# Attention over memory and a feed-forward layer on one core: maxima over tokens without a transposed phi, v behind a weight block, another order table

## The chip, the core and the metric

The kernel runs on one core of a Trainium2 chip. A core has five engines that run their own instruction streams and meet through semaphores: PE (TensorE, matmuls; its weight loads are shown as PEld), DVE (VectorE), ACT (ScalarE), POOL (GpSimd) and SP, which here only issues DMAs. The metric is the device time of one execution in microseconds (us); less is better.

## What is computed

The inputs are q, k, v of shape (8 batches, 8 heads, 576 tokens, 64) and phi of shape (8, 8, 576, 32), all float32 values, and two weights w_in (512 x 2048) and w_out (2048 x 512) that arrive as 8-byte floats.

```
a = exp(phi - max over tokens of phi); a = a / (sum over tokens of a + 1e-9)
k_m = a^T k; v_m = a^T v                       (32 memory rows per head)
attn = softmax over the 32 rows of (q k_m^T / 8)
x = attn v_m, laid out as 4608 tokens x 512
h = x @ w_in; g = h * cos(h); out = g @ w_out
```

## The kernel before

**What is multiplied.** x is never formed. For each batch the kernel folds v_m into w_in (`fold`, `fold_first`, tiles pv, pvf, vf, vw), so that h is attn times the folded weight. `gemm1` makes one 128-row piece of h for a group of 384 tokens (tile hp, L730 for the first group in float32, L739 for the others in float16 pairs), `act` and `act_end` turn it into g (tiles u and gp), `gemm2` multiplies by w_out and sums in three accumulators (tile acc, L776 for the first group, L781 for the others). There are 12 groups of 384 tokens and 16 pieces f per group. PSUM has three buffers for hp, three for acc and two small ones that everything else takes in turn.

**What prepares a batch.** `memory(b)` subtracts the maxima from phi, takes exp, and multiplies with k and v (tile psA, 40 matmuls that use 32 columns of the array); `attend(b)` makes the scores (tile sc), their softmax and its transpose (tile aT). Batch 0 has its own `memory_first`, which first makes k_m (psk), and then v_m (psv, X_v, tpx_v, vm) from a separate load of v.

**The maxima.** There are two ways. For batches 4 to 7 `maximum(b)` (L344 to L353) takes elementwise maxima over the token blocks on DVE, and POOL's `partition_all_reduce` then gives every partition the maximum over all of them. Batches 1 to 3 (`NT = 4`) load a second, transposed copy of phi (tile phiT, 576 KB, L208), DVE reduces it along tokens (nmx, L452), and two PE matmuls spread the result over the partitions (tile top, L455).

**The weights.** They arrive in 8 blocks each (`load_w_in`, `load_w_out`, 1 MB a block). `to_float32` rebuilds a float32 block from the bits of 8-byte floats: a cast of the upper halves on ACT (L277), then one DVE operation that ors in the lower bits (L280), then a square sum on ACT (L283) for the scale. `convert_next` does one or more of these blocks at each step f of group 0, so the first 100 us carry this work beside the matmuls.

**The order.** The program is written in loops, but each engine's stream is reordered at the end: `NEXT` holds one string per engine, and each number says which of the instructions not yet issued comes next. The order of every engine, and that of SP's DMA issues, is therefore a table of numbers. An engine waits at an instruction whose inputs aren't ready, and everything behind it in its table waits too.

PE starts with filler matmuls on zeros (tile warm, L833, 43 of them), which are placed in the opening by the same table.

Of the kernel before, what the change touches and what calls it, by code (L numbers as in the profile page):

```python
# [11 lines left out]
F32 = mybir.dt.float32  # L12
# [32 lines left out]
NT = 4  # L45
# [50 lines left out]
    mybir.EngineType.Activation: (  # L96
# [907 lines left out]
```

## Time and profile before

| | |
|---|---|
| median of 3 runs | 678.17 us (677.82 to 681.54) |
| profiled execution, its own time | 677.69 us |
| its span from first to last instruction | 675.8 us |
| PE busy | 664.4 us, 98% |
| DVE busy | 517.8 us, 77% |
| ACT busy | 496.0 us, 73% |
| POOL busy | 19.9 us, 3% |
| HBM read, written | 51.79 MB, 9.44 MB |

An engine's busy time says how much of the span its units ran, not whether somebody waited for it. The 1.9 us between the span and the execution's own time lie outside the instructions.

### The profile page before, as it was taken

What the parts mean: (1) busy time and instruction counts of PE and PEld (TensorE: products, weight loads), DVE (VectorE), ACT (ScalarE), POOL (GpSimd) and SP (SyncE); (2) the same over time, 40 slices, a digit from 0 to 9 for tenths busy, and PEclk for the clock granted to TensorE, in tenths of its full rate; (3) what the DMA queues carried; (4) which work ended last, traced back from release to release, by engine and by line L of the source; (5) the groups of instructions that cost most, each with busy time, mean ns of one, the idle gap of its engine ahead of it and who ended that gap; (6) DMA issues with size and microseconds to landing.
All of it is one profiled execution on the core that took longest, in us unless ns stands there. A gap on an engine that the chain in (4) does not pass through costs nothing.

```text
span 675.8 us, 12557 instructions
## 1 busy us (share of the span) xinstructions
PE 664.4 (98%) x4959; PEld 345.8 (51%) x4959; DVE 517.8 (77%) x1124; ACT 496.0 (73%) x921; POOL 19.9 (3%) x26
## 2 busy tenths in 40 slices
PE   7799999999999999999999999999999999999997
PEld 3343455564454445665454545655445445665543
DVE  5868799999999877788669877688766766766553
ACT  1798889988878967776866868776775776756553
POOL 4001100000000000000000000000000000000000
PEclk9999999999999999999999999999999999999999
DMA  8997780016143000630027000520000000001001
GB/s 296 396 342 275 241 294 1 18 52 217 42 165 99 32 1 1 194 102 16 1 60 233 18 1 32 179 85 1 32 16 16 17 1 32 16 1 48 16 16 63
DMA packets 25290, 62.03 MB, mean 92 GB/s; under 512 B 2256, under 2 KB 8720, under 8 KB 23184
## 3 DMA queue, kind: packets, MB, share of 16 engines
q1 hardware_dynamic: 20768, 53.24, 23.0%
q10 hardware_dynamic: 4464, 8.00, 3.2%
q8 instruction: 39, 0.64, 0.4%
q14 instruction: 19, 0.16, 0.1%
HBM read 51.79 MB, written 9.44 MB: 91 GB/s over the span
## 4 chain that ended last, share of the span: by engine, by line
PE 97%; ACT 1%; DVE 1%; issue 0%
PE acc L781 51%; PE hp L739 26%; PE acc L776 6%; PE pv L667 3%; PE hp L730 3%; PE psA L479 2%; PE sc L582 2%; PE warm L833 1%; PE pvf L676 1%; PE pv L676 1%; PE psA L485 0%; ACT w_in_sb L277 0%; DVE w_in_sb L200 0%; PE psk L387 0%; PE tpx L503 0%; PE top L455 0%
## 5 line engine op out<-in xcount | busy, mean ns | idle before, releaser
L781 PE MATMUL acc<-wo,gp 128*128 128x512 f16 x1584 | 372.8, 379 | 0.0
L781 PEld LDWEIGHTS <-gp 128*128 128x128 f16 x1584 | 151.2, 98 | 170.6 <-issue 13.9
L739 PE MATMUL hp<-aT,vw 128*128 128x192 f16 (+1 forms) x1440 | 199.0, 283 | 0.0
L739 PEld LDWEIGHTS <-vw 128*128 128x128 f16 x1440 | 130.2, 98 | 71.2 <-issue 5.6
L750 ACT ACTIVATE gp<-hp,cu 128x192 int32<-128x192 f32 (+1 forms) x240 | 115.4, 491 | 59.9 <-PE hp L739 26.5
L751 DVE SCALAR_TENSOR_TENSOR u<-hp,cu,gp 128x192 f32<-128x192 f32 (+1 forms) x240 | 119.1, 504 | 45.4 <-ACT gp L750 43.5
L756 ACT ACTIVATE u<-u,quarter 128x384 f32<-128x384 f32 x192 | 116.2, 612 | 41.4 <-DVE u L751 40.3
L760 DVE SCALAR_TENSOR_TENSOR u<-hp,u 128x384 f32<-128x384 f32 x176 | 96.2, 551 | 36.6 <-ACT u L756 35.3
L763 DVE TENSOR_TENSOR gp<-u,gp 128x384 f16<-128x384 f32 x176 | 95.7, 549 | 27.3 <-ACT gp L762 26.7
L762 ACT CAST gp<-u 128x384 f16<-128x384 f32 x176 | 87.1, 506 | 28.5 <-DVE u L760 25.3
L776 PE MATMUL acc<-wo,gp 128*128 128x512 f32 x96 | 45.5, 603 | 0.0
L683 DVE SCALAR_TENSOR_TENSOR vw<-pv,vw 128x512 f16<-128x512 f32 x48 | 32.5, 683 | 5.9 <-ACT vw L682 5.9
L682 ACT ACTIVATE vw<-pv 128x512 f16<-128x512 f32 x48 | 27.8, 592 | 5.3 <-PE pv L667 5.1
L776 PEld LDWEIGHTS acc<-wo,gp 128*128 128x128 f32 x96 | 17.1, 190 | 20.5 <-issue 17.2
L756 ACT ACT_TABLE_LOAD x20 | 25.7, 1283 | 0.4
L730 PE MATMUL hp<-aT,vf 128*128 128x384 f32 x64 | 24.1, 501 | 0.8 <-DVE aT L613 0.8
L805 ACT ACTIVATE ob<-acc,os 128x512 f32<-128x512 f32 x27 | 18.4, 687 | 4.5 <-PE acc L781 4.0
L588 DVE STREAM_TRANSPOSE at<-sc 128x288 f32<-128x288 f32 (+2 forms) x32 | 14.6, 468 | 4.3 <-PE sc L582 4.2
L730 PEld LDWEIGHTS hp<-aT,vf 128*128 128x128 f32 x64 | 11.3, 189 | 12.4 <-issue 2.6
L667 PE MATMUL pv<-w_in_sb,vp 64*32 64x512 f16 x432 | 15.8, 380 | 0.0
L582 PE MATMUL sc<-q,km 64*32 64x288 f32 (+2 forms) x256 | 14.7, 414 | 0.8 <-DVE vf L703 0.6
L833 PE MATMUL warm<-zeros 128*128 128x512 f16 x43 | 12.4, 425 | 2.3 <-DVE zeros L183 2.3
(159 smaller groups left out, 474.0 us busy)
## 6 DMA issues: line engine op xcount, KB each, us to landing
kv<-in_kv SPq DMA_DIRECT2D x28, 516.0 KB, 7.2
raw_out<-in_w_out SPq DMA_DIRECT2D x8, 1024.0 KB, 6.7
q<-in_qT SPq DMA_DIRECT2D x7, 1152.0 KB, 6.3
out<-ob ACTq DMA_DIRECT2D x30, 256.0 KB, 2.0
raw_in<-in_w_in SPq DMA_DIRECT2D x6, 1024.0 KB, 7.0
phi<-in_phi SPq DMA_DIRECT2D x8, 512.0 KB, 6.3
wo<-in_w_in SPq DMA_DIRECT2D x2, 1024.0 KB, 15.6
kv<-in_kv SPq DMA_DIRECT2D x14, 129.0 KB, 7.2
```

The lines of the kernel that those rows point to most:

```text
L667: nc.tensor.matmul(pv[g][M * c:M * (c + 1)], lhsT=st["vp", b][rows, vi, c], rhs=w2[rows, c, wi], start=(k == 0), stop=(k == 2), skip_group ...
L683: nc.vector.scalar_tensor_tensor(out=vw[:, 1, g], in0=src, scalar=T, in1=vw[:, 0, g], op0=ALU.mult, op1=ALU.subtract)
L730: nc.tensor.matmul(hp[:, :GT], lhsT=st["vf", q][:, g, fo * P:(fo + 1) * P], rhs=st["aTf"][:, g], start=(g == 0), stop=(g == 1))
L739: nc.tensor.matmul(hp[:, c0:c0 + n], lhsT=vw[:, wi, g, fo * P:(fo + 1) * P], rhs=aT[:, ai, g, c1:c1 + n], start=(k == 0), stop=(k == 5))
L750: nc.scalar.activation(ni[:, c], hp[:, c], AF.Copy, scale=cu, bias=0.25)
L751: nc.vector.scalar_tensor_tensor(out=u[:, c], in0=hp[:, c], scalar=cu, in1=ni[:, c], op0=ALU.mult, op1=ALU.subtract)
L756: nc.scalar.activation(u, u, AF.Sin, scale=TWO_PI_BELOW, bias=quarter)
L760: nc.vector.scalar_tensor_tensor(out=u, in0=hp[:, :GT], scalar=2.0 ** -17, in1=u, op0=ALU.mult, op1=ALU.mult)
L762: nc.scalar.copy(gp[:, 0], u)
L763: nc.vector.tensor_tensor(out=gp[:, 1], in0=u, in1=gp[:, 0], op=ALU.subtract)
L776: nc.tensor.matmul(accs[grp][t], lhsT=gp[:, t * P:(t + 1) * P], rhs=wo[:, f + 1], start=(f == 0), stop=(f == NF - 1))
L781: nc.tensor.matmul(accs[grp][t], lhsT=gp[:, gi, t * P:(t + 1) * P], rhs=parts[:, wi], start=(f == 0 and gi == 0 and wi == 0), stop=(f == N ...
```

## The change

The diff without the order tables, of which the first row of PE's stands for all (all five tables are new):

```diff
-NT = 4
 LAG = 4
 NEXT = {
     mybir.EngineType.PE: (
-        "0x26 8 0x16 1x8 2x8 3x8 6x2 18x5 6x2 7 6 7 6 0 6 5 9x4 0 8x9 0 7x6 9x16 0x14 1 2 0x3 1 0 14x2 6x6 7 "
+        "0x26 8 0x16 1x8 0x10 1x8 0x7 1 2 0 2 0x7 24x2 0x40 2x2 0x3 1 0 1 0x10 8x2 16 0x2 1 0x2 11 0x4 1 2 3 "
...
     def load_phi(b):
-        if 0 < b < NT:
-            loads["phiT", b] = t = ld.tile([P, 2, S], F32, tag="phiT", name=f"phiT_{b}", bufs=1)
-            nc.sync.dma_start(out=t, in_=phiT[b].rearrange("(g p) s -> p g s", p=P))
...
-        cast = nc.scalar.copy(top, upper)
+        cast = nc.scalar.copy(top, upper) if j > 0 else nc.vector.tensor_copy(out=top, in_=upper)
...
     def memory(b):
-        a = loads.pop(("phi", b))
-        if b < NT:
-
-            nmx = wk.tile([P, 2], F32, tag="nmx", name=f"nmx_{b}", bufs=1)
-            nc.vector.tensor_reduce(out=nmx, in_=loads.pop(("phiT", b)), op=ALU.max, axis=AX.X)
-            top = small_ps(f"top_{b}")[:, 0:HM]
-            for g in range(2):
-                nc.tensor.matmul(top[:, g * P:(g + 1) * P], lhsT=nmx[:, g:g + 1].broadcast_to([P, P]), rhs=ident,
-                                 start=True, stop=True)
-        else:
-            top = st["top", b]
-        yield
-        if b >= NT:
+        a = loads["phi", b]
+        if ("top", b) not in st:
+            maximum(b)
+        top = st["top", b]
+        loads.pop(("phi", b))
+        yield
+        if b > 1:
             yield
             yield
...
     load_q(0)
+    load_w_in(0)
     load_first(v_first, H * K1, H * KV)
-    load_w_in(0)
     load_w_in(1)
...
-            if i == e - 6 and NT <= b + 1 < B:
+            if i == e - 6 and ("phi", b + 1) in loads:
                 maximum(b + 1)
```

So all of batches 1 to 7 take `maximum(b)`; three DMAs, three DVE reductions and six PE matmuls go; three times four DVE operations and one all-reduce come. The cast of block 0 of each weight moves from ACT to DVE (`j > 0` is the condition for ACT). The load of w_in's block 0 is issued ahead of the five loads of the first batch's v.

**DVE around the first block of w_out.** The names: raw_in and raw_out are weight blocks as loaded, w_in_sb and wo the rebuilt ones, vf is the folded weight of batch 0 copied from its PSUM tile pvf, u and gp the activation of piece f of group 0. Before:

```order
L280 SCALAR_TENSOR_TENSOR w_in_sb<-raw_in_122,w_in_sb 128x4x256
L751 SCALAR_TENSOR_TENSOR u_0_391<-hp_0_388,gp_0_392 128x384
L703 COPY vf_315<-pvf_1_347 128x256
L280 SCALAR_TENSOR_TENSOR wo<-raw_out_125,wo 128x1024
L758 TENSOR_TENSOR gp_0_392<-hp_0_388,u_0_391 128x384
```

With the change:

```order
L275 SCALAR_TENSOR_TENSOR w_in_sb<-raw_in_122,w_in_sb 128x4x256
L740 SCALAR_TENSOR_TENSOR u_0_389<-hp_0_386,gp_0_390 128x384
L272 CAST wo<-raw_out_125 128x1024
L275 SCALAR_TENSOR_TENSOR wo<-raw_out_125,wo 128x1024
L692 COPY vf_315<-pvf_1_347 128x256
L747 TENSOR_TENSOR gp_0_390<-hp_0_386,u_0_389 128x384
```

The copy of vf, which frees a small PSUM buffer, stood ahead of the w_out block's work and now stands behind both of its operations.

**DVE at the maxima of batch 1.** phi is the block of batch 1, at the scores of batch 0, mx the maxima. With the change:

```order
L740 SCALAR_TENSOR_TENSOR u_2_466<-hp_2_463,gp_2_467 128x384
L342 TENSOR_TENSOR mx_434<-phi_360 128x512
L275 SCALAR_TENSOR_TENSOR w_in_sb<-wo,w_in_sb 128x4x256
L343 TENSOR_TENSOR mx_434<-mx_434 128x256
L346 TENSOR_TENSOR mx_434<-mx_434,phi_360 64x128 x2
L586 TENSOR_TENSOR at_232<-at_232,rm_233 128x384
L457 TENSOR_TENSOR phi_360<-phi_360,mx_434 64x128
L692 COPY vf_401<-pvf_1_452 128x512
L452 TENSOR_TENSOR phi_360<-phi_360,mx_434 128x1024
L457 TENSOR_TENSOR phi_360<-phi_360,mx_434 64x128
L747 TENSOR_TENSOR gp_2_467<-hp_2_463,u_2_466 128x384
```

The first subtraction from phi waits for POOL's all-reduce of mx, and the copy of vf, the large subtraction and the product gp of piece 2 stand behind it.

**PE at the memory products of batch 1.** hp are pieces of group 0, psA the products of phi with k and v, on 32 columns of the array. Before (the first 16 products stand ahead of these rows):

```order
L730 MATMUL hp_5_611<-aT_231,vf_403 128x384 x2
L479 MATMUL psA_0_473<-kv_2_370,phi_362 32x129 x4
L479 MATMUL psA_1_474<-kv_2_370,phi_362 32x129 x4
L479 MATMUL psA_1_474<-kv_3_372,phi_362 32x129 x4
L479 MATMUL psA_0_473<-kv_3_372,phi_362 32x129 x4
L485 MATMUL psA_0_473<-kv_4_374,phi_362 32x129 x2
L485 MATMUL psA_1_474<-kv_4_374,phi_362 32x129
L485 MATMUL psA_0_473<-kv_4_374,phi_362 32x129 x2
L485 MATMUL psA_1_474<-kv_4_374,phi_362 32x129
L730 MATMUL hp_6_647<-aT_231,vf_403 128x384 x2
L485 MATMUL psA_1_474<-kv_4_374,phi_362 32x129 x2
```

With the change:

```order
L719 MATMUL hp_5_610<-aT_231,vf_401 128x384
L468 MATMUL psA_0_472<-kv_0_364,phi_360 32x129 x4
L468 MATMUL psA_0_472<-kv_1_366,phi_360 32x129 x4
L468 MATMUL psA_0_472<-kv_2_368,phi_360 32x129 x4
L468 MATMUL psA_0_472<-kv_3_370,phi_360 32x129 x4
L474 MATMUL psA_0_472<-kv_4_372,phi_360 32x129 x4
L468 MATMUL psA_1_473<-kv_0_364,phi_360 32x129 x4
L468 MATMUL psA_1_473<-kv_1_366,phi_360 32x129 x4
L468 MATMUL psA_1_473<-kv_2_368,phi_360 32x129 x4
L468 MATMUL psA_1_473<-kv_3_370,phi_360 32x129 x4
L474 MATMUL psA_1_473<-kv_4_372,phi_360 32x129 x4
L719 MATMUL hp_6_646<-aT_231,vf_401 128x384 x2
```

The 40 products stood in three pieces with hp matmuls between them and now stand in one. In the same way the 16 score products of batch 1 go from three pieces to two, and the eight pvf products of the third quarter of w_in from two to one.

## Rows read from the trace of the kernel before

**Rows 1.** Page, busy time, share of the span and instructions per engine.

```profile
PE 664.4 (98%) x4959; PEld 345.8 (51%) x4959; DVE 517.8 (77%) x1124; ACT 496.0 (73%) x921; POOL 19.9 (3%) x26
```

**Rows 2.** Stretches: length, then PE, PEld, DVE, ACT, POOL busy; granted clock; DMA, GB/s.

```profile
20.00:25.00 5.00, 2.44 (x24) 0.91 (x22) 4.60 (x8) 3.43 (x7) 0.00 (x0) 1.00 1.04 417
35.00:40.00 5.00, 5.00 (x23) 2.45 (x29) 4.32 (x9) 4.76 (x10) 0.00 (x0) 1.00 1.06 337
40.00:50.00 10.00, 10.00 (x113) 4.78 (x100) 5.43 (x13) 8.92 (x15) 0.00 (x0) 1.00 0.92 353
```

**Rows 3.** Chain that ended last, 19 to 50 us: start, length, what.

```profile
26.82 1.24 ACT wo L277
...
30.29 0.55 PE sc L582 x14
...
32.33 1.29 PE warm L833 x6
...
37.49 0.44 PE top L455 x4
```

**Rows 4.** Timeline of the opening: start, busy us, what [idle before <-releaser].

```profile
2.30 4.83 PE L833 MATMUL warm<-zeros 128*128 128x512 f16 x14 [2.30 <-DVE zeros L183]
...
5.43 3.07 SPq L236 DMA_DIRECT2D kv<-in_v_first  x5
...
9.18 1.00 SPq L261 DMA_DIRECT2D raw_in<-in_w_in  x2
```

**Rows 5.** DMA issues at 8.0 to 9.7 us: size, us from issue to landing.

```profile
kv<-in_v_first SPq DMA_DIRECT2D x1, 128.0 KB, 7.5
...
raw_in<-in_w_in SPq DMA_DIRECT2D x1, 1024.0 KB, 10.0
```

**Rows 6.** Groups by line (L751: first 50 us): busy us, mean ns | idle before.

```profile
L277 ACT CAST wo<-raw_out 128x1024 f16<-128x1024 bf16 x8 | 10.8, 1347 | 0.0
L280 DVE SCALAR_TENSOR_TENSOR wo<-raw_out,wo 128x1024 uint32<-128x1024 uint32 x8 | 9.8, 1220 | 4.3 <-ACT wo L277 4.2
L200 DVE MEMSET w_in_sb<- 128x1024 f32 x3 | 2.7, 912 | 0.5 <-issue 0.5
L751 DVE SCALAR_TENSOR_TENSOR u<-hp,gp 128x384 f32<-128x384 f32 x6 | 3.2, 552 | 0.2 <-ACT gp L750 0.2
L703 DVE COPY vf<-pvf 128x256 f32<-128x256 f32 x2 | 0.8, 404 | 0.2 <-PE pvf L676 0.2
```

**Rows 7.** Groups by line and shape, the two ways to the maxima.

```profile
L452 DVE TENSOR_REDUCE nmx<-phiT 128x2 f32<-128x1152 f32 x3 | 4.0, 1332 | 0.0
L352 POOL PARTITION_ALL_REDUCE mx<-mx x4 | 4.3, 1072 | 95.4 <-DVE mx L351 95.4
```

**Rows 8.** Timeline of POOL, its first all-reduce.

```profile
50.58 0.35 POOL L441 PARTITION_ALL_REDUCE l<-l  x1 [41.88 <-DVE l L439]
```

**Rows 9.** Timeline of PE, 48 to 82 us: pieces on 32 columns.

```profile
48.69 0.41 PE L485 MATMUL psA<-kv,phi 64*32 64x129 f32 x4
...
53.52 0.71 PE L582 MATMUL sc<-q,km 64*32 64x288 f32 x16
...
55.02 1.14 PE L582 MATMUL sc<-q,km 64*32 64x288 f32 x14
...
58.94 0.67 PE L582 MATMUL sc<-q,km 64*32 64x288 f32 x2
...
61.45 1.08 PE L676 MATMUL pvf<-w_in_sb,vm 64*32 64x512 f32 x14
...
63.52 1.04 PE L676 MATMUL pvf<-w_in_sb,vm 64*32 64x512 f32 x2
...
80.41 1.09 PE L676 MATMUL pvf<-w_in_sb,vm 64*32 64x512 f32 x16
```

**Rows 10.** Timeline of PE, two whole fold groups of 24 matmuls.

```profile
183.35 0.84 PE L667 MATMUL pv<-w_in,vp 64*32 64x512 f16 x24
...
438.64 1.27 PE L667 MATMUL pv<-w_in_sb,vp 64*32 64x512 f16 x24
```

More of the change, by code (lines that the diff above doesn't have):

```diff
@@ L49 @@
     mybir.EngineType.PE: (
[46 rows of a table removed]
-    mybir.EngineType.Activation: (
[18 rows of a table removed]
-    mybir.EngineType.DVE: (
[24 rows of a table removed]
[44 rows of a table added]
+    mybir.EngineType.Activation: (
[18 rows of a table added]
+    mybir.EngineType.DVE: (
[25 rows of a table added]
     mybir.EngineType.Pool: (
-        "1 3x2 1x2 0x2 1x3 0x12 "),
+        "1 0x2 2 4 0 3 1 0 1x2 0x14 "),
     mybir.EngineType.SP: (
-        "0x36 6 0x2 4 0x3 1x2 0x9 3x2 0x8 3x2 0x8 3x2 0x8 3x2 0x8 3x2 0x14 "),
+        "0x35 6 0x3 3x2 0 2 0x8 3x2 0x8 3x2 0x8 3x2 0x8 3x2 0x8 3x2 0x14 "),
 }
@@ L165, in attention_then_ffn @@
 @with_exitstack
-def attention_then_ffn(ctx: ExitStack, tc: tile.TileContext, phi, phiT, kv, k_first, v_first, qT, w_in, w_out, eye, out):
+def attention_then_ffn(ctx: ExitStack, tc: tile.TileContext, phi, kv, k_first, v_first, qT, w_in, w_out, eye, out):
     nc = tc.nc
@@ L963, in attention_then_ffn @@
     issue_in_order(tc)
-_INS = ["phi", "phiT", "kv", "k_first", "v_first", "qT", "w_in", "w_out", "eye"]
+_INS = ["phi", "kv", "k_first", "v_first", "qT", "w_in", "w_out", "eye"]
 def kernel(**inputs):
@@ L981 @@
         "phi": np.ascontiguousarray(phi.transpose(0, 2, 1, 3)).reshape(B, S, HM),
-        "phiT": np.ascontiguousarray(phi[:NT].transpose(0, 1, 3, 2)).reshape(NT, HM, S),
         "kv": kv.reshape(B, S, H * KV),
```

173 rows, old and new, of the table NEXT are left out of this document.

## The prediction

> **What bounds the kernel now.** I read the busy shares first: PE is busy for 664.4 of 675.8 us [rows 1], so no other engine's saving counts unless it lets PE start sooner or work less. The stretches tell where the missing 11.4 us lie: PE runs 2.44 of 5 us between 20 and 25, but all of 35 to 40 and of 40 to 50 [rows 2]; from there to the tail it has no gap that matters. The chain that ended last says what holds PE in the opening: up to 30.3 us it runs through the weight conversion on ACT, with the cast of w_out's block 0 (1.24 us at 26.82) as a link, then through the scores' second half at 30.29 and PE's own fillers at 32.33, and after that through PE alone [rows 3]. So the time is the opening plus PE's stream. The change can win by a shorter opening, by matmuls that go, and by a cheaper order of those that stay; it can lose by new waits on PE, most of all behind DVE, which gets work in the opening.
>
> The sum is made against the profiled execution's own 677.69 us, 0.48 below the median of 678.17 and 0.13 below the fastest timed run. What is about 0.5% here, 3.4 us, is all that a measurement of this kernel can tell from no change.
>
> **The opening.** The block of w_in landed at 19.2 us (issue at 9.18, 10.0 to landing), the last of v at 15.5 (the five issues end at 8.5, the last one starts at about 8.0 and takes 7.5) [rows 4, 5]. The same bytes go through the same queue in another order, so the block comes about 3.5 us sooner and the last of v at about 19.2. Each of the two is one of the inputs of the first fold, and the later one only changes its name. ACT loses its cast of that block but has to wait for v's products, so I let the first piece's conversion gp_0 end where it ended before, at 26.82, when ACT took up the cast of w_out's block [rows 3]. From there DVE's new order counts: u (0.55), the new cast, the operation that ors in the lower bits (1.22) and the copy of vf (0.40) [rows 6], since the scores' second half takes the PSUM buffer which that copy frees, and it stands behind all four.
>
> The cast on DVE has no row. From below: DVE's memset of an equal tile, which reads nothing, 0.91; from above: ACT's cast, 1.35, while DVE's own operation with two inputs of that size takes 1.22 [rows 6]. A cast reads one input, so I take 1.05, between the two DVE rows. [...]
>
> So the copy ends at 26.82 + 0.55 + 1.05 + 1.22 + 0.40 and some 0.1 of handing over, 30.1, and the scores run at about the time they did (30.29 [rows 3]), but all of them and not the second half alone: +0.3. Then the six fillers that stood at 32.33 (1.29 us [rows 3]) no longer stand in PE's way; they now run ahead of the first hp, in a wait that exists anyway: -1.3. **Opening: -1.0** (bounds: -1.9, with the cast at 0.7 and a shorter ACT path, to +1.0, with the cast at 1.35 and the copy a further handing over late).
>
> **Matmuls that go.** The six top matmuls hold PE 0.44 us per batch [rows 3], three times: **-1.3**. The three DMAs (576 KB each) and the three DVE reductions cost PE nothing: in the opening the queue is full anyway (DMA share 1.0 [rows 2]) and phi now lands sooner.
>
> **Pieces that are joined.** [...] Batch 1's scores take 0.71 + 1.14 + 0.67 in three pieces, where one undivided group takes 0.71: as two groups they save 1.1. The third quarter's pvf takes 1.08 + 1.04 in two pieces, undivided 1.09: 1.0. The last psA piece is 4 of 80 passes and takes 0.41, so nearly 0.3 is its change-over; two of these go: 0.6 [rows 9]. The ends of neighbouring pieces overlap by up to 0.1 in these rows, so of 2.7 I take **-2.4** (bounds -2.7 and -1.5, if half of the long pieces was waiting that comes back).
>
> **New waits.** DVE has the second cast (1.05) and, for batch 1, four operations on phi in place of one reduction of 1.33 [rows 7], about 0.3 more. Between 35 and 40 it was busy 4.32 of 5 us [rows 2], so this work delays what is behind it. Then it halts at the subtraction until POOL's all-reduce (1.07 [rows 7]) is done, with the copy of vf, the large subtraction and the product gp of piece 2 queued behind. The product frees the hp buffer that piece 5 needs: PE waits there. Lower bound 0, since DVE idles 4.57 of the 10 us from 40 to 50 [rows 2]; upper bound the halt on top of the work, 2.4. I take the work alone: **+1.4**. Batches 2 and 3 pay the same 0.3 on DVE and the all-reduce where POOL is otherwise idle: nothing for PE. The two zeroing memsets on POOL that now queue behind its first all-reduces are of the last w_in blocks, which are converted late: nothing.
>
> **Later.** One fold group of 24 matmuls took 1.27 us where the others take 0.84 [rows 10]; that wait needn't come back in the new order: **-0.4** (bounds -0.8 and +0.8: each order splits three such groups, and the new one splits one psA group as well). The last matmuls and stores keep their form: 0.
>
> **The sum:** -1.0 - 1.3 - 2.4 + 1.4 - 0.4 = -3.7, so 674.0 for the profiled execution; medians lie a little above it, and I say **674.2**, 0.6% under the median of before.
>
> **The rivals.** *DVE takes the bound of the opening.* It has the two casts, and in-order waits on it hold PE in two places. Price: the opening gives nothing (+1.0 against my sum), the new waits take their upper bound (+1.0 more): 676.2. For it: DVE ran 4.60 of 5 us from 20 to 25 [rows 2]. Against it: its 4.57 idle us after 40.
>
> [...]
>
> *Slower: the first all-reduce isn't ready.* POOL's first all-reduce stood at 50.58 and had waited long for its input [rows 8]; nothing shows from when POOL could have run it. Now DVE halts for one at about 38 (my estimate: 26.82 and what stands on DVE up to there). [...] Against it: POOL has 19.9 us of work in the whole span [rows 1], so it has time to get ready.
>
> **How the numbers follow.** The forecast 0.55 (0.02 of it within 0.5%), the DVE rival 0.30 (0.02 of it slower), the clock 0.08, the all-reduce 0.07. Faster by over 0.5%, below 674.8: 0.53; within 0.5%: 0.02 + 0.28 + 0.08 = 0.38; slower: 0.09. The range 671.5 to 678.2 holds the lower bounds of the opening and of the waits (a further -2.3 and the rest), the DVE rival and the clock, and leaves out the all-reduce and the ends of the others. The forecast's own range is 671.5 to 674.8.
>
> **What would show it.** Right: the scores' second half near 30.2, no filler between hp and the first acc, acc's first matmul ahead of 34.3 with four hp pieces done, a wait of PE at piece 5's hp below 2 us, one psA piece of about 2.4 us. Wrong: the DVE cast above 1.35 or PE gaps after 45 us; a granted clock below 1 in the first 30 us; DVE idle at the first subtraction from phi for more than 2 us.

## The result, and the profile after

The changed kernel takes **672.0 us** (median of 4 executions, 671.76 to 673.61) against 679.01 (median of 4, 677.82 to 681.54) of the kernel before: ratio 0.9897, 95% interval 0.9863 to 0.9931. It is faster by 1.0%. Forecast were 674.2 and a range of 671.5 to 678.2. The two medians hold executions in which TensorE's granted clock fell (a mean of 0.997 in after's 673.61; before's 679.86 and 681.54 lie near its executions beside the experiments that have 0.997 and 0.992); with the clock kept, at a mean of 0.999 or 1.000, before took 677.58 to 678.67 (median 677.85, from the executions timed beside the experiments) and after 671.76 to 672.03, so 5.9 of the 7.0 us between the medians are won without it.

| | before | after |
|---|---|---|
| profiled execution, its own time | 677.69 us | 673.61 us |
| its span | 675.8 us | 671.5 us |
| the other executions | 677.82 to 681.54 | 671.76 to 672.03 |
| PE busy | 664.4 us | 661.4 us |
| HBM read | 51.79 MB | 50.02 MB |

The profiled execution of after is the slowest of its four, by 1.7 us. The stretches of 1 us show why (columns: length, PE busy, granted clock, DMA share, GB/s):

```profile
20.00:21.00 1.00, 0.25 (x1) 1.00 1.19 393
21.00:22.00 1.00, 0.65 (x10) 1.00 1.01 409
22.00:23.00 1.00, 1.00 (x17) 0.59 1.00 418
23.00:24.00 1.00, 1.00 (x3) 0.50 1.01 418
...
25.00:26.00 1.00, 1.00 (x4) 0.70 1.00 401
```

The granted clock went from 1.00 to 0.50 at about 22.2 us and came back at about 25.6. In the profiled execution of before the same place had a clock of 1.00 with less work on PE: 2.44 of the 5 us from 20 to 25 [rows 2], where after has 3.90. PE's timeline shows what stood there (start, busy us, what, idle before and its releaser):

```profile
21.69 1.24 PE L665 MATMUL pvf<-w_in_sb,vm 64*32 64x256 f32 x16 [0.35 <-ACT vm L425]
22.86 2.74 PE L822 MATMUL warm<-zeros 128*128 128x512 f16 x6
25.39 2.21 PE L719 MATMUL hp<-aT,vf 128*128 128x384 f32 x6
...
30.38 0.56 PE L571 MATMUL sc<-q,km 64*32 64x192 f32 x16 [0.80 <-DVE vf L692]
```

The six fillers took 2.74 us where six took 1.46 before in the same view (1.29 up to the start of the next matmul [rows 3]), and the first hp stands behind them. DVE's part of the opening in the same execution:

```profile
15.63 0.77 DVE L272 CAST w_in_sb<-raw_in 128x1024 f16<-128x1024 bf16 x1
...
27.99 0.73 DVE L272 CAST wo<-raw_out 128x1024 f16<-128x1024 bf16 x1
...
38.58 0.28 DVE L457 TENSOR_TENSOR phi<-phi,mx 64x128 f32<-64x128 f32 x1 [0.96 <-POOL mx L347]
```

The two casts take 0.77 and 0.73. At the first subtraction DVE waits 0.96 for POOL, whose first all-reduce runs as soon as its input is there:

```profile
37.20 1.35 POOL L347 PARTITION_ALL_REDUCE mx<-mx  x1 [30.28 <-DVE mx L346]
```

The pieces on 32 columns, the counterparts of [rows 9], in PE's timeline:

```profile
41.56 0.91 PE L719 MATMUL hp<-aT,vf 128*128 128x384 f32 x2 [0.19 <-DVE gp L747]
42.40 1.09 PE L468 MATMUL psA<-kv,phi 128*32 128x129 f32 x32
43.42 0.42 PE L474 MATMUL psA<-kv,phi 64*32 64x129 f32 x8
...
50.95 0.73 PE L571 MATMUL sc<-q,km 64*32 64x288 f32 x16
...
53.96 0.72 PE L571 MATMUL sc<-q,km 64*32 64x288 f32 x16
...
58.24 1.09 PE L665 MATMUL pvf<-w_in_sb,vm 64*32 64x512 f32 x16
```

Piece 5's hp waits 0.19. The scores take 0.73 + 0.72 where they took 0.71 + 1.14 + 0.67, and the third quarter's pvf takes 1.09 in one piece. Last, the view of PE's waits from 40 us on (engine and line, what it waited for, us in total, times, longest). The kernel before has no row in this view from 45 us on; after has four, and the first three lie behind 270 us:

```profile
PE hp L728 <- DVE u L749: 0.6, 2, 0.4
PE tpx L492 <- DVE X L487: 0.3, 1, 0.3
PE pv L656 <- ACT gp L739: 0.2, 1, 0.2
PE hp L719 <- DVE gp L747: 0.2, 1, 0.2
```

### The profile page after: what moved, and what is told of

The parts are those of the page before. It is cut to its first block, busy times and chain, and to the rows that moved or that the text cites. A ratio compares the mean times of both kernels' runs of the same rounds, so it can differ in the third digit from the quotient of the medians.

```text
span 671.5 us, 12541 instructions
## 1 busy us (share of the span) xinstructions
PE 661.4 (98%) x4947; PEld 343.8 (51%) x4947; DVE 517.3 (77%) x1135; ACT 492.2 (73%) x919; POOL 24.3 (4%) x29
## 3 DMA queue, kind: packets, MB, share of 16 engines
q1 hardware_dynamic: 19952, 51.47, 22.2%
HBM read 50.02 MB, written 9.44 MB: 89 GB/s over the span
## 4 chain that ended last, share of the span: by engine, by line
PE 90%; ACT 4%; DVE 3%; issue 1%; DMA 1%; POOL 0%; SPq 0%; ACTq 0%; DVEq 0%; POOLq 0%
PE acc L770 49%; PE hp L728 24%; PE acc L765 6%; PE pv L656 3%; PE hp L719 2%; PE psA L468 2%; PE sc L571 2%; PE warm L822 1%; ACT u L745 1%; DMA phi<-in_phi 1%; PE pv L665 1%; ACT L745 1%; ACT gp L739 1%; DVE u L740 1%; PE pvf L665 0%
## 5 line engine op out<-in xcount | busy, mean ns | idle before, releaser
L751 ACT CAST gp<-u 128x384 f16<-128x384 f32 x176 | 86.5, 506 | 24.0 <-DVE u L749 23.1
L822 PE MATMUL warm<-zeros 128*128 128x512 f16 x43 | 13.8, 469 | 1.2 <-DVE zeros L181 1.2
L347 POOL PARTITION_ALL_REDUCE mx<-mx x7 | 8.4, 1203 | 167.1 <-DVE mx L346 167.1
```

Source lines behind the costliest of these rows:

```text
L751: nc.scalar.copy(gp[:, 0], u)
```

## Experiments

All times are medians of 5 to 12 executions. e1_fill to e4_tops are built on the changed kernel. From e5_halves on the kernel of e1_fill is the base, since its clock fell in none of its executions; differences are taken against its median, 671.98. It was not timed again beside the later ones.

### The clock: more fillers, and none

e1_fill has five more fillers on PE, e2_nofill eight fewer:

```diff
 PE order, e1_fill
 warm<-zeros x2
+warm<-zeros x4
 tpx_v<-ident,X_v x2
+warm<-zeros
 pvf_0<-w_in_sb,vm x8
 PE order, e2_nofill
 sc_0_0<-q,km x8
-warm<-zeros x6
 psv<-kv,phi x40
-warm<-zeros x2
 tpx_v<-ident,X_v x2
```

> The changed kernel with five more fillers on PE: four ahead of tpx_v, one ahead of the first pvf, in waits of 0.91 and 0.35 us that stand there. Theory (the clock): the profiled execution of the changed kernel (673.61) lies 1.7 above the mean of its three timed ones (671.9) because the granted clock was 0.72 from 20 to 25 us: six fillers took 2.74 us there and the first pvf 1.24. With the waits filled the clock stays at 1.00, the six fillers take 1.3 to 1.5, the first hp starts near 24.6 and not at 25.4, and all executions lie at 671.9, within 0.4. Rival: the clock falls without regard to these waits, or the 1.7 has another cause: then some executions still lie at 673 and above.

> The changed kernel without the eight fillers that stand between 16.4 and 19.8 us (six after the first scores, two ahead of tpx_v). Theory (the clock): PE now has waits of 1.3 us around psv as well, the granted clock falls in every profiled and timed execution, and the median is 673.4 to 674.5. Rival: the clock does not hang on these fillers: median 671.9, granted clock 1.00 in 20 to 25 us.

Measured: e1_fill **671.98** (671.83 to 672.34, ratio 0.9884, interval 0.9868 to 0.9900), e2_nofill **673.61** (673.09 to 674.29, ratio 0.9909, interval 0.9895 to 0.9922). The stretches of e1_fill (length; PE, PEld, DVE, ACT, POOL busy; clock, DMA share, GB/s), then those of e2_nofill:

```profile
20.00:25.00 5.00, 4.87 (x34) 1.98 (x33) 4.86 (x9) 3.79 (x8) 0.00 (x0) 1.00 1.06 409
```

```profile
20.00:25.00 5.00, 4.19 (x25) 1.62 (x26) 4.58 (x9) 3.35 (x8) 0.00 (x0) 0.66 1.05 408
```

The theory holds on both sides: with the waits filled no execution lies above 672.34, without fillers none below 673.09, and the difference is 1.6 us. So here the clock went with what PE has to do while it waits for v: the mean granted clock was 1.000 in all five executions of e1_fill and 0.995 to 0.997 in all six of e2_nofill. The kernel as changed stands between: it fell in one execution of four (0.997), and in one of five of e4_tops, which has no added fillers (0.997). With the five fillers the mean clock was 0.999 or more in all executions of e1_fill, e5_halves, e6_in_act, e8_v_first, e10_joined, e11_products and e12_sum, but 0.997 in three of six of e7_out_act and in one of six of e9_best. Where it fell there no kept trace shows.

The kernel before loses clock more often than its profiled execution (677.69, mean clock 0.999) lets one think. Of its 54 executions timed beside the experiments, the 19 with a mean granted clock of 0.999 or 1.000 took 677.58 to 678.67, the 14 with 0.996 or 0.997 took 678.71 to 679.95, and the 21 with 0.992 took 680.53 to 681.45. In which stretch it falls no kept trace shows. So a ratio to the median of before holds a part that is the clock's, and the differences to 671.98 are the ones to read.

The undisturbed opening is seen in e1_fill's timeline of PE:

```profile
29.15 0.56 PE L572 MATMUL sc<-q,km 64*32 64x192 f32 x16 [0.81 <-DVE vf L693]
29.64 2.85 PE L720 MATMUL hp<-aT,vf 128*128 128x384 f32 x8
32.33 3.60 PE L766 MATMUL acc<-wo,gp 128*128 128x512 f32 x8
```

The scores' second half starts at 29.15 and not at 30.38, and acc at 32.33 with all four hp pieces done.

### The matmuls that go: six of their kind put back

```diff
         psA = [small_ps(f"psA_{b}_{g}") for g in range(2)]
+        if b < 4:
+            for g in range(2):
+                nc.tensor.matmul(psA[g][:, 256:256 + P], lhsT=quarter.broadcast_to([P, P]), rhs=ident,
+                                 start=True, stop=True, skip_group_check=True)
```

> The changed kernel with six added float32 matmuls of 128x128, two ahead of the psA of each of batches 1 to 3, of the form of the removed top matmuls; they write a part of psA's PSUM tiles that nothing reads, and the maxima stay as they are. Theory (PE is the bound, so each pair costs its 0.44 us): +1.3, 673.2 against 671.9. Rival (some of them fall into waits that PE has anyway): +0.5 or less.

Measured: **673.26** (673.12 to 674.27, ratio 0.9906, interval 0.9890 to 0.9921), so +1.28 against e1_fill. (This kernel does not have the five fillers, but its granted clock in the profile was 1.0, and the undisturbed executions of after lie at 671.9, from where it is +1.3 too.) Between the traces of e1_fill and e4_tops all that stands behind a pair moves by 0.44, three times. So the matmuls that left this kernel's full PE gave their whole time, 0.44 a pair.

### The joined pieces: split again, and others split elsewhere

e3_split undoes the joining of batch 1's pieces, the rest of the new order staying:

```diff
 PE order, e3_split
 hp_5
-psA x40
-hp_6 x2
+psA x16
+hp_5
+psA x22
+hp_6 x2
+psA x2
...
-sc_288 x8
-acc x4
-pvf_5 x8
-acc
+sc_288 x7
+acc x3
+sc_288
+acc
+pvf_5 x7
+acc
+pvf_5
```

> The changed kernel with the pieces of batch 1 on 32 columns split as they were before: psA in three pieces, the second half of the scores in 7 and 1 products, the third quarter's pvf in 7 and 1. Theory (a change-over between full matmuls and those on 32 columns costs PE time): +2.4, so 674.3 against 671.9, with the sc pieces giving 1.1 of it, pvf 1.0, psA 0.3 to 0.6. Rival (the long pieces of before were waits for inputs, which this order does not have): +0.5 or less, 672.4 or below.

Measured: **679.55** (678.48 to 681.8, ratio 0.9996, interval 0.9983 to 1.0010): +7.6 against e1_fill, far above both. The six of its twelve executions that kept the clock took 678.48 to 678.9, which is +6.5 to +6.9. PE's timeline of the profiled one, which did not keep it:

```profile
45.46 0.41 PE L474 MATMUL psA<-kv,phi 64*32 64x129 f32 x4
46.81 0.30 PE L492 MATMUL tpx<-ident,X 128*128 128x128 f32 x1 [0.94 <-DVE X L487]
47.85 1.12 PE L765 MATMUL acc<-wo,gp 128*128 128x512 f32 x2 [0.74 <-DVE wo L275]
...
48.98 4.37 PE L765 MATMUL acc<-wo,gp 128*128 128x512 f32 x6
...
56.28 0.71 PE L571 MATMUL sc<-q,km 64*32 64x288 f32 x14
...
59.69 0.67 PE L571 MATMUL sc<-q,km 64*32 64x288 f32 x2
...
62.96 1.09 PE L665 MATMUL pvf<-w_in_sb,vm 64*32 64x512 f32 x14 [1.55 <-DVE w_in_sb L275]
...
65.04 1.04 PE L665 MATMUL pvf<-w_in_sb,vm 64*32 64x512 f32 x2
```

The three added pieces take 0.41, 0.67 and 1.04, 2.1 together; psA's 0.41 costs nothing on balance, since its pieces come to 1.02 + 1.39 + 0.41 = 2.82 from start to start and the one piece of e1_fill to 2.81. PE's waits for DVE and ACT that e1_fill does not have come to 3.9 (1.55 at pvf, 0.94 at tpx, 0.74 at acc and 0.68 at hp), and behind those at tpx and acc the granted clock falls for a while (0.59 from 49 to 53 us, 1.00 behind it): six acc records took 4.37 where the same six take 2.74, another 1.6. So the experiment does not give the price of the pieces alone. It shows that they cannot be undone alone: the last two psA products stand behind hp_6 and hold back X, for which the transposes wait.

A row in it speaks against my reading of [rows 9], though: 2 records took 0.67, 14 took 0.71. The time of a piece hardly hangs on the number of its products. e5_halves tests that where nothing waits:

```diff
 PE order, e5_halves (one such place in each of batches 2 to 7)
 sc x4
-sc x4
 hp (or acc)
+sc x4
 hp (or acc)
```

> The kernel of e1_fill (671.98) with one group of eight score products (16 records) in each of batches 2 to 7 split into two pieces of four, with one full matmul of the neighbouring piece between them; these stand where DVE and ACT have slack. First theory (mine of the prediction: a change-over of nearly 0.3 us, the rest of a piece's time in proportion to its products): six change-overs, +1.8, 673.8. Second theory (eight products of 32 columns and 64 rows stand on eight different parts of the array and run at the same time, so a piece of four takes as long as one of eight: in e3_split 2 records took 0.69 us, 14 took 0.73, 16 took 0.74): each split costs a whole further piece, 0.69 to 0.74, six times, +4.1 to +4.4, 676.2.

Measured: **676.05** (675.87 to 676.87, ratio 0.9952, interval 0.9935 to 0.9968), +4.07. One of the six places, two halves and behind them an undivided group (the 16 score products of a batch leave 32 records in the trace, so four products are x8):

```profile
204.21 0.69 PE L572 MATMUL sc<-q,km 64*32 64x288 f32 x8
204.83 0.34 PE L729 MATMUL hp<-aT,vw 128*128 128x384 f16 x1
205.09 0.69 PE L572 MATMUL sc<-q,km 64*32 64x288 f32 x8
...
206.63 0.71 PE L572 MATMUL sc<-q,km 64*32 64x288 f32 x16
```

Eight records take 0.69 and sixteen 0.71. So the price is the second theory's: a group that is split pays nearly its whole time once more, 0.68 per split (4.07 / 6). That the products of a group run side by side on different parts of the array is my reading of these times; whether a part of the 0.68 is the change from one kind of matmul to the other no run here separates.

e10_joined joins three later fold groups that the new order issues in two pieces:

```diff
 PE order, e10_joined
-pv_2_2 x12
 acc, hp x15
+pv_2_2 x12
 pv_2_2 x12
```

> The kernel of e1_fill with three later fold groups, which its order issues in two pieces (12 and 12 products, 6 and 18, 8 and 16), issued in one, the first piece moved to the place of the second. By the second theory of e5_halves a split costs a whole further pass through the array: the six pieces take 0.64, 0.64, 0.43, 0.85, 0.44 and 0.65 us, three undivided groups 0.87 each, so -1.0 in all, 671.0. Rival (the pieces filled waits of PE, which come back): 671.7 or above.

Measured: **671.43** (671.28 to 671.76, ratio 0.9883, interval 0.9861 to 0.9904), -0.55. Less than that is the groups': in the traces e10_joined is 0.54 ahead of e1_fill (both profiled executions kept the clock) before its first edit already, 0.72 behind the first joined group, 0.88 behind the second and 0.89 behind the third. So some 0.35 of the expected 1.0 came. A wait of 0.18 us behind the first joined group took a part back; why the third gave nothing no row shows.

### The casts of the first blocks

e6_in_act and e7_out_act each put one of the two casts back on ACT:

```diff
 ACT order, e6_in_act
 km_0<-tpx_k
+CAST w_in_sb<-raw_in
 at_0<-at_0 (exp)
 ACT order, e7_out_act
 gp_0<-hp_0
+CAST wo<-raw_out
 u_0<-u_0 (sine, with its table load)
```

> The kernel of e1_fill with the cast of block 0 of w_in back on ACT, placed where ACT idles for 4.7 us (after km, ahead of the first exp of the scores). Theory (DVE holds the opening, as the DVE rival of the prediction has it: its chain from 14.6 to 24.7 us has no gap): the 0.77 us of the cast leave the chain, the first hp stands 0.5 to 0.8 earlier, and the time falls by 0.4 to 0.8, to 671.2 to 671.6. Rival (v's path through ACT holds the first fold as long): no change, 672.0, within 0.2.

> The kernel of e1_fill with the cast of block 0 of w_out back on ACT, behind the conversion of gp_0, where it stood before the change. Theory (the cast took ACT's time ahead of the activation table load and the first sine, and DVE's OR waits for it anyway): the first sine comes 1.3 later, DVE's products behind it too, the scores' second half at about the same time, and acc starts 0.2 to 1.0 later: 672.2 to 673.0. Rival (DVE is the bound there too): the copy of vf comes earlier and the time falls by 0.3 or more.

Measured: e6_in_act **671.87** (five executions from 671.78 to 672.0; a sixth took 3786.14, and no row tells why; ratio 0.9890, interval 0.9865 to 0.9914), no change; e7_out_act **673.62** (672.77 to 673.96, ratio 0.9913, interval 0.9888 to 0.9938), +1.64. This median mixes two levels: three executions kept the clock (672.77, 672.82 and the profiled 673.36: +0.8 to +1.4), three had a mean clock of 0.997 (673.88 to 673.96). The cast's own price is that of the first three. The number of e6_in_act is its rival's, but the reason is not. DVE's timeline of e6_in_act:

```profile
16.34 1.05 DVE L578 STREAM_TRANSPOSE at<-sc 128x384 f32<-128x384 f32 x2 [0.94 <-PE sc L572]
```

Without the cast DVE waits 0.94 for the first scores, where with it it had no gap: the cast ran in that wait and cost nothing. I had called the chain gapless because the cast filled it. In e7_out_act ACT's cast takes 1.33 at 26.15, ahead of the table load (1.28 at 27.50); its copy of vf, behind both, comes late, and the scores' second half falls apart:

```profile
29.13 0.53 PE L572 MATMUL sc<-q,km 64*32 64x192 f32 x8 [0.79 <-DVE vf L693]
30.10 0.53 PE L572 MATMUL sc<-q,km 64*32 64x192 f32 x8 [0.44 <-ACT vf L692]
30.56 2.85 PE L720 MATMUL hp<-aT,vf 128*128 128x384 f32 x8
```

The hp behind them starts 0.9 later than in e1_fill (29.64), which is the price that the timed executions show. Of the two casts the one of w_out is the one that pays.

### The order of the first loads

```diff
-    load_w_in(0)
     load_first(v_first, H * K1, H * KV)
+    load_w_in(0)
 DVE order
-CAST w_in_sb<-raw_in
 at_0, rm_0 (transposes, maxima and their subtraction)
+CAST w_in_sb<-raw_in
 SCALAR_TENSOR_TENSOR w_in_sb<-raw_in,w_in_sb
```

> The kernel of e1_fill with the loads of the first batch's v ahead of w_in's block 0 again, and DVE's cast of that block moved behind the maximum subtraction of the scores, since the block lands some 4 us later. Theory of the prediction (each of the two is an input of the first fold and the later one only changes its name): same, 671.7 to 672.5. Rival (the early block lets DVE do the cast in a place where nothing else is ready): the cast lies on the chain now and the time rises by 0.6 to 1.0, to 672.6 to 673.0.

Measured: **672.63** (672.26 to 673.81, ratio 0.9903, interval 0.9880 to 0.9926), +0.65, at the border of the two ranges. DVE's timeline decides for the rival: DVE waits 0.94 for the first scores again, and the cast stands on the chain behind them:

```profile
19.18 0.75 DVE L273 CAST w_in_sb<-raw_in 128x1024 f16<-128x1024 bf16 x1
```

The early block is what lets the cast run in DVE's wait.

### The halt for the all-reduce

```diff
 DVE order, e11_products
+gp_2<-hp_2,u_2
+u_3<-hp_3,gp_3
 phi<-phi,mx (64 rows)
 vf_1<-pvf
 phi<-phi,mx
 phi<-phi,mx (64 rows)
-gp_2<-hp_2,u_2
-u_3<-hp_3,gp_3
```

> The kernel of e1_fill (671.98) with DVE's product of piece 2 and the operation on u of piece 3 moved from behind the three subtractions from phi to ahead of them, into the 0.96 us in which DVE waits for POOL's all-reduce. Theory of the prediction (the halt for the all-reduce, with the product behind it, costs PE +1.4 at piece 5's hp): the time falls by 1.0 to 1.4, to 670.6 to 671.0. Rival (PE has matmuls in hand and pays only what the trace shows, 0.18 us at that hp): 671.8 to 672.0.

Measured: **671.48** (671.28 to 672.54, ratio 0.9883, interval 0.9859 to 0.9906), -0.50: between the two. DVE's wait for POOL and PE's 0.18 at piece 5's hp are gone from the profile. Against e1_fill the first psA starts 0.84 earlier (40.33 for 41.17), of which 0.55 stood there before the edit, so 0.3 is the edit's. The profiled execution is the slowest of its six (672.54), and its own rows show a reason: ACT's cast of w_out's block 2 waits 0.73 for its load (0.24 in e1_fill), and the first scores behind it take 1.44 in place of 0.73.

### Two attempts at more

e9_best joins what the experiments suggested, and e12_sum what was left of it:

```diff
 e9_best
-        (nc.vector if x < 3 * WS else nc.gpsimd).memset(w_in_sb[:, :, x:x + WS], 0.0)
+        (nc.vector if x < 2 * WS else nc.gpsimd).memset(w_in_sb[:, :, x:x + WS], 0.0)
 PE order
-hp_1
+hp_1 x2
 pvf_1 x8 (in one piece)
 psA_0, psA_1 (in turn)
 DVE order
+vf<-pvf_1
 SCALAR_TENSOR_TENSOR wo<-raw_out,wo
-vf<-pvf_1
 ACT order
-raw_in_0<-w_in_sb (square)
 gp_0, u_0, vf, gp_1, CAST, u_1
+raw_in_0<-w_in_sb (square)
```

> The kernel of e1_fill with all of these: POOL in place of DVE zeroes w_in's third block (0.91 us off DVE's chain ahead of the first scores), three fillers fewer ahead of the first hp, the second fold piece pvf in one piece behind the first four hp matmuls, DVE's copy of vf ahead of the OR of w_out's block 0, ACT's first square behind the second sine and its copy of vf ahead of gp_1's conversion, the products of e11_products ahead of the subtractions, and batch 1's psA with both halves in turn (its eight products on 64 rows at the same time). Theory (DVE and the split pieces hold the opening, the order of psA costs 2.84 against 2.38 us): -0.5 from psA, -0.5 from the joined pvf piece, -0.5 to -1.0 from the opening: 670.0 to 670.6. Rival (ACT, without a gap from 23 to 39 us, takes the bound): 671.3 to 671.8, psA's share alone.

Measured: **672.23** (671.96 to 673.95, ratio 0.9897, interval 0.9875 to 0.9920), +0.25. PE's first acc starts at 30.82 and not at 32.33, so the opening gained its 1.5 us. The view of PE's waits from 26 us on tells where they went, in rows that e1_fill does not have or has smaller:

```profile
PE pvf L665 <- DVE w_in_sb L275: 0.7, 1, 0.7
...
PE psA L468 <- ACT phi L454: 0.5, 1, 0.5
PE hp L719 <- DVE gp L747: 0.4, 1, 0.4
```

0.7 + 0.5 + 0.4 is the gain, given back by 45 us. ACT waits 0.45 for a block of w_in at 28.47 and from there has its casts, squares and sines without a gap up to 39 us; that PE, started earlier, meets this is my reading of it. The time lies above the rival's range too (671.3 to 671.8), so even psA's share was not kept.

Of e12_sum's edits, ACT's order:

```diff
 ACT order, e12_sum
+km_1<-tpx x2
+gp_5<-hp_5
 CAST wo<-raw_out (block 2)
 three squares
-km_1<-tpx
-gp_5<-hp_5
-km_1<-tpx
```

> The kernel of e1_fill (671.98) with the edits of e11_products (671.48) and e10_joined (671.43), batch 1's psA with both halves in turn, and the way from psA to the scores of batch 1 freed of the weights that e9_best left in it: DVE's second X operation ahead of the two ORs of w_out's blocks 1 and 2, ACT's two km copies and the conversion of gp_5 ahead of the cast of w_out's block 2 (that block landed 0.2 to 0.7 us late there), and PE's two tpx matmuls behind hp_5 together. Theory (the edits lie at different places and each counts where PE is the bound): 0.5 and 0.5 as measured and 0.46 of psA, 670.5. Rival (as in e9_best, group 0's weight work holds PE a little later, and psA's share comes back as a wait): 670.9 to 671.2.

Measured: **673.78** (673.48 to 674.11, ratio 0.9915, interval 0.9895 to 0.9935), +1.8: a miss by more than the whole gain. ACT now halts at km_1 for PE's transpose (ACT's timeline), and PE pays further on (its own timeline):

```profile
46.90 0.27 ACT L497 ACTIVATE km<-tpx 64x128 f32<-64x128 f32 x1 [2.56 <-PE tpx L492]
```

```profile
58.15 1.09 PE L665 MATMUL pvf<-w_in_sb,vm 64*32 64x512 f32 x16 [1.44 <-DVE w_in_sb L275]
```

I had taken a wait for a load (0.2 to 0.7 us) out of ACT's stream and put one of 2.56 in. So the versions that beat the changed kernel are the small ones: e10_joined (671.43) and e11_products (671.48), each some 0.5 us under after's 672.0 and with a clock that holds. By their traces 0.3 of it is the edits'; the fastest executions of before differ by 0.2 between the two sets of runs (677.87 beside e1_fill, 677.64 beside these). The two were not run together alone.

## Why the prediction was right, and where it was not

The time came out 2.2 under the forecast and inside the range, faster as forecast. The terms did less well than the sum. The ledger takes e1_fill's profiled execution (672.34) against that of before (677.69), both with the clock kept, as starts of the same instructions on PE:

| term | forecast | measured | from |
|---|---|---|---|
| opening | -1.0 | -2.4 | hp of piece 2 starts at 29.64 in place of 30.78, and no six fillers (1.3) behind it |
| matmuls that go | -1.3 | -1.3 | e4_tops, +1.28 |
| pieces joined | -2.4 | -3.0 | sc -1.1, pvf -1.0, psA -0.2, the matmul behind each of four pieces -0.1; -0.3 more at a pvf that was in one piece before too (1.34 at 39.59 before, 1.09 now) |
| new waits | +1.4 | +0.2 | idle of 0.18 at piece 5's hp |
| later | -0.4 | +1.2 | from 72 us to the end the lead shrinks by 0.3, with 0.9 of the tops won in it |
| sum | -3.7 | -5.3 | 677.69 to 672.34 is -5.35 |

The opening, the pieces and the waits came out 1.4, 0.6 and 1.2 better than forecast and the last term 1.6 worse, so that the sum is off by only 1.6 is in part luck: errors of both signs stand in it. The opening's figure is good to some 0.5: in the profiles of e1_fill, e5_halves, e10_joined, e11_products and e12_sum, which share it, gp_0 starts between 25.21 and 25.76, and e1_fill's is the latest.

*The opening* was wrong at one step: "I let the first piece's conversion gp_0 end where it ended before". Without the cast ACT was ready sooner, waited 0.17 for PE's first hp, and in e1_fill gp_0 ends at 26.25, not 26.82 (-0.57). The cast of w_out's block took 0.74 and not 1.05 (-0.3), and the four DVE operations overlap a little where I had put 0.1 of handing over (DVE's timeline of e1_fill):

```profile
26.29 0.56 DVE L741 SCALAR_TENSOR_TENSOR u<-hp,gp 128x384 f32<-128x384 f32 x1 [0.38 <-ACT gp L740]
26.76 0.74 DVE L273 CAST wo<-raw_out 128x1024 f16<-128x1024 bf16 x1
27.54 1.23 DVE L276 SCALAR_TENSOR_TENSOR wo<-raw_out,wo 128x1024 uint32<-128x1024 uint32 x1
28.68 0.42 DVE L693 COPY vf<-pvf 128x256 f32<-128x256 f32 x1
```

My bounds for the cast, 0.91 to 1.35, left out the truth: the memset of the same tile (0.91) was no lower bound for it, since the casts on DVE took 0.73 and 0.77 in after and 0.74 to 0.78 in e1_fill, e6_in_act, e7_out_act, e8_v_first and e9_best. The 0.7 in the opening's bound of -1.9 stands in no row of before; those are the times that the runs showed in its place. That the order of v and w_in's block "only changes its name" was wrong too: it is worth 0.65 (e8_v_first), since it decides whether the cast of w_in's block costs anything.

*The matmuls that go* came out as forecast.

*The pieces joined* had nearly the right size (-2.7 for the joined ones) from a wrong mechanism. A change-over of nearly 0.3 at each piece, with the rest of a piece's time in proportion to its products, would have made e5_halves cost 1.8; it cost 4.07. No run shows such a change-over by itself; what the runs show in its place is that a split costs 0.68, nearly the 0.71 of the whole group. For psA my reading failed: "the last psA piece is 4 of 80 passes and takes 0.41, so nearly 0.3 is its change-over" promised 0.6 and gave 0.2, because the new order issues all of psA_0 ahead of psA_1, so that the eight 64-row products of the last block no longer stand together: 2.74 us in all with 0.42 for eight of their records twice, where in e9_best the two in turn take 1.97 + 0.45. So do those of batch 3 in e1_fill itself, all sixteen records together:

```profile
190.12 0.45 PE L475 MATMUL psA<-kv,phi 64*32 64x129 f32 x16
```

*The new waits* failed at "I take the work alone: +1.4". DVE did wait 0.96 for the all-reduce and the product did stand behind it, but PE had hp pieces and acc matmuls in hand and paid 0.18. The removal of the halt gave 0.50, of which the trace shows 0.3 (e11_products), so the place was right and the price about a third of what I took, or less.

*Later* had the wrong sign. The wait of 1.27 at a fold group [rows 10] did come back, split in two, at 432 us, with a wait of 0.23 between the parts, and the new order has three waits of its own, of 0.27, 0.18 and 0.40 (PE's timeline of e1_fill). PE gaps after 45 us were one of my signs of being wrong, and these are such gaps:

```profile
432.47 0.39 PE L657 MATMUL pv<-w_in_sb,vp 64*32 64x512 f16 x1
433.09 0.84 PE L657 MATMUL pv<-w_in_sb,vp 64*32 64x512 f16 x23 [0.23 <-ACT gp L740]
```

```profile
271.51 0.50 PE L493 MATMUL tpx<-ident,X 128*128 128x128 f32 x2 [0.27 <-DVE X L488]
...
273.18 1.15 PE L729 MATMUL hp<-aT,vw 128*128 128x192 f16 x12 [0.18 <-DVE u L750]
...
492.49 1.14 PE L729 MATMUL hp<-aT,vw 128*128 128x384 f16 x6 [0.40 <-DVE u L750]
```

*The rivals.* The fall of the clock, given 0.08, occurs in one execution of four at 1.6, and its rows (a granted clock of 0.59 and 0.50 at 22 to 25 us) are among those that I had named as a sign of error. In after's fall the six fillers took 2.74 for 1.46 and the pvf ahead of them 1.24 for 0.94 (e1_fill), 1.6 together. The fall follows 2 us with 0.25 and 0.65 us of work on PE, but the profiled execution of before had 0.52, 0.23 and 0.53 in the three from 20 to 23 us and kept its clock at 1.00. That was one execution: 35 of the 54 timed later had a mean clock of 0.997 or less, so its rows at 20 to 25 us [rows 2] prove little for the others. Had only the profiled execution been timed, 673.6 would have looked like a hit on 674.0, with the clock's 1.6 standing in for what the terms missed. DVE as the bound of the opening did not come true at its price: the opening gave 2.4, not nothing, and PE paid 0.18 at piece 5's hp. A part of it is so all the same, since PE's wait of 0.81 ahead of the scores' second half still ends with DVE's copy of vf. The first all-reduce ran at 37.20, as soon as its input was there, and DVE waited 0.96 for it, so the slower rival had no ground.

## What to carry to other kernels

Half of a group of eight small products took 0.69 us here and the whole group 0.71 (e5_halves), so count pieces, not products, and issue a group whole; but move it whole only if nobody waits for its first half. A wait in the trace is room for work that has to be done anyway, and an instruction moved to another engine is worth what that engine then waits for: one cast was worth nothing, the other about 1 us. Where two engines are both near their limit, an opening made faster can be paid back some microseconds later, as in e9_best; follow the lead at marks along the program (start of the same matmul in both traces) before a gain is believed. And one profiled execution does not tell how often a clock falls: the mean clock of every timed execution does.

## What was not expected of the hardware

A piece of float32 products on 32 columns took 0.41 to 0.45 us at 129 columns, 0.67 to 0.74 at 288 and 1.04 to 1.09 at 512, nearly the same for 2, 8, 14 or 16 records; longer ones are 1.14 at 288 and 1.34 at 512 in before and 1.44 at 288 in e11_products. TensorE's granted clock fell to 0.50 in after with no idle gap of PE above 0.91 us in the 14 us ahead of it, in an execution whose stretch from 15 to 20 us was 97% busy (4.84 of 5 us), though some 2.8 us of that were products on 32 columns (scores and psv); with five fillers more, of about 0.25 us each (six took 1.47), it stayed up, at a mean of 0.999 or more, in every execution of e1_fill, and of six kernels built on it, but not of e7_out_act and e9_best (0.997 in three of six and in one of six).
